# Norm and weight decoding ranked three pairs later, and new assumed durations, in the written order of an attention and MLP kernel

## The chip, the cores and the metric

The kernel runs on one core of one Trainium2 chip. The metric is the device time of one execution in microseconds (us); lower is better. Before the change it was 1068.26 us, the median of 3 runs (1066.97 to 1068.33).

## The reference

Causal attention in blocks of 64 over 8 batches, 8 heads, 576 positions and 64 values a head, followed by a norm over 512 channels and a two-layer MLP with a residual:

```python
scores = np.matmul(q, k.transpose(0, 1, 3, 2)) / np.sqrt(D)
scores = np.where(pos[:, None] // 64 >= pos[None, :] // 64, scores, -1e9)
attn = np.exp(scores - scores.max(-1, keepdims=True))
attn = attn / (attn.sum(-1, keepdims=True) + 1e-09)
x = (attn @ v).transpose(0, 2, 1, 3).reshape(B, S, 512)
xn = (x - mean(x)) / np.sqrt(var(x) + 1e-06) * g_ln
out = x + np.maximum(xn @ w_ch1, 0.0) @ w_ch2      # 512 -> 2048 -> 512
```

Everything is float32. The MLP weights come to the core as 64-bit words.

## The kernel before, in words

**Attention.** The 64 combinations of batch and head are worked as 32 pairs of two heads. A pair loads `raw` (q and k, L385) and `v` (L386). TensorE makes the scores (L396); VectorE masks them, takes the row minimum and writes them to SBUF (`soften`, L411); ScalarE takes the exponential (L414); TensorE transposes the result (L423); VectorE or ScalarE copies the transposes out of PSUM as `pt` (L217 and L215, the two branches of one helper); TensorE multiplies with `v` (L429, L433); VectorE turns the product (`ot`, L506) and SyncE stores it to `xd` (L508). The first 64 positions of eight pairs are worked together by `first` (L543 to L586), once in eight pairs. At the end of each batch `recip` (L515, L516) inverts the sums.

**Norm.** `norm_tiles` takes two 128x512 tiles of `x` at a time. For each it loads four parts from `xd` (L621, L627), multiplies them by the inverted sums (L636, on VectorE or GpSimd), stores the tile to `xrow` (L640), and takes mean and variance (`stats`, L645, L646). For both together it computes the inverse root (`guess` on VectorE, L654 to L657; `newton` on GpSimd, L663 to L666). Then the tile is centred (L671), multiplied by `g_sb` on GpSimd (L674), transposed (L676), stored to `xw` in four parts (L680) and loaded back as `xt` (L684).

**Decoding.** `decode` loads a block of weight words (`wr`, L325 and L327), rebuilds the floats on ScalarE (L330, L335), GpSimd (L333) and VectorE (L339, L342) and stores them: those of the first layer to `w1f` (L358), those of the second, split into a high and a low part, to `wcs` (L354). There are 16 blocks of each layer.

**MLP.** The 36 tiles of 128 rows are worked in rounds of 8, 8, 8, 8 and 4. In a round, 8 groups of weights follow each other. A group's first layer is seven products (L814), which TensorE works from `xm` (seven operand arrays, made in `operands`, L701 and L712) and from the weight tiles `wa` and `wb`. ScalarE copies a product out (`t`, L822), VectorE adds another to it (L827), ScalarE and VectorE write the high and the low part of the rectified result `h` (L833, L834). The second layer is one job of six matmuls and six more for each tile (`y`, L874, with the weights `wc`); VectorE adds it to `ya` (L883). In the first round a group's `wa` and `wb` are made from `w1f`: SyncE loads `wf` (L765), GpSimd makes sums and differences (`sum`, L773), ScalarE, VectorE and GpSimd split them (L784; copies at L215 and L217), and SyncE stores them to `was` and `wbs` for the later rounds (L792). `wc` is loaded from `wcs` (L758). In this text group 7 is the last of the first round. The operands of the second round overwrite those of the first, each after its last product of group 7 has read it.

**What sets the order.** Nothing runs when it is ready: the order of each of the five engines is written once, at build time, and every engine then works its instructions strictly in that order. `Plan.run` keeps a list of tasks with assumed durations. On each engine it takes, of the tasks whose inputs and buffers it believes ready, the one of the lowest `prio`. Pair k has `prio` 100 + 10k and a little more. A block of decoding has that of pair 12 + 0.97n (n counts the blocks), a norm step of the first round that of pair 10 + 3q, the operands of the first round that of pair 22, the norm of the second round that of pair 31.2, the MLP's own vector work 0 or 1, the operands of later rounds 2. SyncE issues every transfer, and so is such an engine too. A transfer is believed to land after its bytes at `BW`, a `LAG` and a `TAIL`. Buffers come from shared pools with a limit for each name: `x`, a norm tile, has 2 of the 21 places of the pool `small`.

Of the kernel before, what the change touches and what calls it, by code (L numbers as in the profile page):

```python
# [18 lines left out]
P = 128  # L19
LATS = {'PE': .2, 'ACT': .23, 'DVE': .21, 'POOL': .13, 'SP': 0}  # L20
SWITCH = {64: .2, 128: .1, 1: .05, 2: .15}
OWN = {'PE': .0, 'ACT': .2, 'DVE': .2, 'POOL': .1, 'SP': 0}
BW, LAG, TAIL = 3.0e5, .65, 1.5
BIAS = {'PE': 0, 'SP': 0, 'DVE': 0, 'ACT': 0, 'POOL': 0}
# [4 lines left out]
D_0, D_1 = 12.0, .97  # L29
LN_0, LN_1 = 10, 3  # L30


# [150 lines left out]
def attn_mlp_kernel(ctx: ExitStack, tc: tile.TileContext, qk, qk0, v, v0, w1, w2, g, out):  # L183
# [91 lines left out]
    new_mag, new_sgn = (small(n, [P, 512], I32, 2) for n in ("mag", "sgn"))  # L275
    new_ya, new_x, new_xnt = (small(n, [P, 512], F32, k) for n, k in (("ya", 10), ("x", 2), ("xnt", 2)))
    new_t, new_tt, new_sum = small("t", [P, 512], F32, 4), small("tt", [P, 2, 2, P], F32, 4), small("sum", [P, 2, 256], F32, 2)
# [97 lines left out]
    def pair(k):  # L375
# [135 lines left out]
        if c == 3:  # L511
            rs, whole = Buf(), sums_all[:, b].rearrange("p i c h -> p (i c h)")

            def recip():
                nc.vector.tensor_scalar_add(whole, whole, 1e-9)  # L515
                nc.vector.reciprocal(whole, whole)  # L516
            add("DVE", .4, recip, r=batch_sums[b], w=[rs], prio=pr())
            xparts[b].append(rs)
# [79 lines left out]
    for j in range(NJ):  # L598
        for second in (False, True):
            decode(j, second, 100 + 10 * (D_0 + D_1 * n), [ends[min(int(D_0 + D_1 * n) - 3, NPAIR - 1)]])  # L600
            n += 1
# [7 lines left out]
    def norm_tiles(n, q, prio, gate):  # L609
# [4 lines left out]
        for h in range(2):  # L614
            t = FROM[n] + ROUNDS[n] // 2 * h + q
            m, r = divmod(t, 9)
            x = new_x()
            part = [Buf(parent=x) for _ in range(4)]
# [25 lines left out]
            def stats(x=x, st=st, h=h):  # L644
                nc.vector.bn_stats(out=st.t[:, 0:6], in_=x.t)  # L645
                nc.vector.bn_aggr(out=norm.t[:, 2 * h:2 * h + 2], in_=st.t[:, 0:6])  # L646
            add("DVE", .85, stats, r=part, w=[mv, st], prio=prio)
            mvs.append(mv)
# [3 lines left out]
        def guess():  # L652
# [4 lines left out]
            nc.vector.tensor_scalar(out=yi, in0=yi, scalar1=-1, scalar2=0x5f3759df, op0=ALU.mult, op1=ALU.add)  # L657
        add("DVE", .45, guess, r=mvs, w=[seed], prio=prio)

# [229 lines left out]
    for n in range(len(ROUNDS)):  # L889
        for q in range(ROUNDS[n] // 2):  # L890
            norm_tiles(n, q, 100 + 10 * (LN_0 + LN_1 * q) if n == 0 else END + 2 * n - 10,
                       gate if n else [ends[int(LN_0 + LN_1 * q) - 2]])
        operands(n, 100 + 10 * (LN_0 + LN_1 * 4) if n == 0 else 2)
        for gp in range(GROUPS):
# [64 lines left out]
```

## Time and profile before

| | before |
|---|---|
| median of 3 runs | 1068.26 us |
| the profiled execution's own time | 1064.36 us |
| its span, first to last instruction | 1062.6 us |
| granted TensorE clock, mean | 0.998 |
| TensorE busy | 1044.1 us (98%) |
| VectorE busy | 786.5 us (74%) |
| ScalarE busy | 450.4 us (42%) |
| GpSimd busy | 294.9 us (28%) |
| moved by DMA | 248.91 MB, 234 GB/s |

The span is the time between the first and the last instruction in one profiled execution; that execution's own time is 1.76 us longer, and the median of the unprofiled runs 3.90 us longer than that. In the lines of the profile PE is TensorE, PEld its loading of weights, DVE VectorE, ACT ScalarE, POOL GpSimd and SP SyncE (SPq: its queue of transfers). "out<-in" names the tiles, "x6" counts instructions. Square brackets hold the idle time of an engine before an instruction and what ended it.

### The profile page before, as it was taken

How to read it: one execution, taken by the hardware profiler on the slowest of the kernel's cores; microseconds unless marked ns; L12 is line 12 of the kernel's file. 1: busy time of each engine (PE TensorE's matmuls, PEld its weight loads, DVE VectorE, ACT ScalarE, POOL GpSimd, SP SyncE). 2: the span in 40 equal slices, each digit the busy share in tenths (PEclk: the TensorE clock that was granted, in tenths of full speed). 3: DMA queues.
4: the chain of work that ended last, by engine and by line, in shares of the span. 5: the costliest groups of instructions: out<-in, count | busy, mean ns of one | idle time of the engine just before them, and what ended most of it. 6: DMA issues, size and time to landing. Idle time of an engine off the chain costs nothing.

```text
span 1062.6 us, 17838 instructions
## 1 busy us (share of the span) xinstructions
PE 1044.1 (98%) x6240; PEld 841.2 (79%) x6240; DVE 786.5 (74%) x1724; ACT 450.4 (42%) x1101; POOL 294.9 (28%) x442
## 2 busy tenths in 40 slices
PE   9999999999999999989999999999999999999998
PEld 6777767667678888778888888888888888888897
DVE  6878998998988899795676694676686665465554
ACT  7768979879864333242121141122133112222221
POOL 0002546533535766270222240221221220000000
PEclk9999999999999999999999999999999999999999
DMA  5448898998969898877777657778657775436873
GB/s 189 154 135 242 224 286 285 294 297 286 336 221 325 252 321 292 255 231 255 207 233 235 202 185 243 232 206 259 185 176 238 264 203 211 163 109 217 317 282 125
DMA packets 237930, 248.91 MB, mean 234 GB/s; under 512 B 159376, under 2 KB 188048, under 8 KB 227600
## 3 DMA queue, kind: packets, MB, share of 16 engines
q1 hardware_dynamic: 237840, 247.77, 71.7%
q8 instruction: 49, 0.80, 0.3%
q14 instruction: 41, 0.34, 0.1%
HBM read 182.71 MB, written 65.01 MB: 233 GB/s over the span
## 4 chain that ended last, share of the span: by engine, by line
PE 63%; DVE 2%; DMA 1%; POOL 0%; issue 0%; DVEq 0%
PE y L874 34%; PE p L814 29%; DMA wc<-wcs 1%; DVE ya L883 0%; DVE t L827 0%; DVE h L834 0%; DVE xm L712 0%; POOL x L674 0%; POOL tt L701 0%; DVE xnt L676 0%; DVE wb L784 0%; DVE tt L701 0%; POOL wb L784 0%; DVE xm L217 0%; POOL xm L712 0%
## 5 line engine op out<-in xcount | busy, mean ns | idle before, releaser
L874 PE MATMUL y<-wc,h 128*128 128x512 f32 x1728 | 434.1, 390 | 1.0 <-ACT h L833 0.8
L874 PEld LDWEIGHTS y<-wc,h 128*128 128x128 f32 x1728 | 321.8, 188 | 68.0 <-DVE h L834 1.8
L883 DVE TENSOR_TENSOR ya<-y,ya 128x512 f32<-128x512 f32 x288 | 197.0, 685 | 152.0 <-PE y L874 150.1
L814 PE MATMUL p<-xm,wa 128*128 128x512 f32 (+1 forms) x960 | 221.4, 368 | 0.0
L814 PEld LDWEIGHTS p<-xm,wa 128*128 128x128 f32 x960 | 170.0, 188 | 31.7 <-ACT sgn L335 0.2
L833 ACT ACTIVATE h<-t 128x512 fp32r<-128x512 f32 (+1 forms) x120 | 62.3, 580 | 276.2 <-DVE t L827 265.9
L814 PE MATMUL p<-xm,wb 128*128 128x512 f32 (+1 forms) x720 | 166.2, 368 | 2.7 <-DVE wb L784 2.5
L814 PEld LDWEIGHTS p<-xm,wb 128*128 128x128 f32 x720 | 127.5, 188 | 27.3 <-DVE wb L784 3.0
L822 ACT COPY t<-p 128x512 f32<-128x512 f32 (+1 forms) x120 | 65.4, 545 | 193.3 <-PE p L814 182.2
L827 DVE TENSOR_TENSOR t<-p,t 128x512 f32<-128x512 f32 (+1 forms) x120 | 75.8, 632 | 42.8 <-PE p L814 38.9
L396 PE MATMUL s<-raw 64*128 64x192 f32 (+4 forms) x640 | 96.4, 435 | 2.1 <-DMA raw<-qk 1.4
L414 ACT ACTIVATE pab<-pab,nm 128x576 f32<-128x576 f32 (+1 forms) x128 | 91.4, 722 | 9.0 <-DVE nm L411 8.8
L396 PEld LDWEIGHTS s<-raw 64*128 64x128 f32 x640 | 60.7, 186 | 38.8 <-issue 29.1
L411 DVE CUSTOM_DVE_ANT_0 pab<-s,never 128x576 f32<-128x576 f32 (+1 forms) x128 | 83.6, 682 | 3.4 <-PE s L396 3.0
L414 ACT ACTIVATE pu<-pu,nm 128x320 f32<-128x320 f32 (+1 forms) x128 | 64.3, 505 | 38.8 <-DVE nm L411 38.7
L433 PE MATMUL o<-pt,v 128*64 128x256 f32 (+1 forms) x768 | 80.3, 344 | 0.0
L333 POOL TENSOR_SCALAR mag<-mag 128x512 f32<-128x512 f32 x32 | 51.2, 1603 | 102.8 <-ACT mag L330 100.9
L834 DVE SCALAR_TENSOR_TENSOR h<-t,h 128x512 fp32r<-128x512 f32 (+1 forms) x120 | 75.4, 675 | 4.7 <-ACT h L833 4.6
L433 PEld LDWEIGHTS o<-pt,v 128*64 128x64 f32 x768 | 56.9, 137 | 26.0
L423 PE MATMUL tr<-ident,pab 128*128 128x128 f32 x512 | 66.1, 279 | 4.9 <-DVE nm L411 2.6
L215 ACT COPY pt<-tr 128x512 f32<-128x512 f32 (+1 forms) x126 | 65.0, 579 | 3.1 <-PE tr L423 2.7
L423 PEld LDWEIGHTS tr<-ident,pab 128*128 128x128 f32 x512 | 57.2, 142 | 9.8 <-DVE pt L217 3.3
(89 smaller groups left out, 982.5 us busy)
## 6 DMA issues: line engine op xcount, KB each, us to landing
wc<-wcs SPq DMA_DIRECT2D x40, 1024.0 KB, 6.7
wa<-was SPq DMA_DIRECT2D x32, 1024.0 KB, 6.6
wb<-wbs SPq DMA_DIRECT2D x32, 768.0 KB, 5.9
raw<-qk SPq DMA_DIRECT2D x32, 576.0 KB, 4.9
wr<-w SPq DMA_DIRECT2D x32, 512.0 KB, 6.5
v<-v SPq DMA_DIRECT2D x32, 320.0 KB, 5.4
x<-xd SPq DMA_DIRECT2D x144, 64.0 KB, 3.5
xrow<-x SPq DMA_DIRECT2D x36, 256.0 KB, 3.8
```

The source lines that it names most:

```text
L215: e.copy(out=out, in_=in_)
L396: nc.tensor.matmul(x, raw.t[HALF[h], 0, col], raw.t[HALF[h], 1, at:at + x.shape[1]], start=True, stop=True)
L411: add("DVE", dve(n) + .01, lambda: nc.vector.tensor_tensor_reduce(out=p.t[:, part(i, h)], in0=s.t[:, cols], in1=hide, scale=-0.125, scalar ...
L414: add("ACT", act(n, True) + .14, lambda: nc.scalar.activation(out=p.t[:, part(i, h)], in_=p.t[:, part(i, h)], func=AF.Exp, bias=nm.t[:, at ...
L423: nc.tensor.transpose(o.t[:, n * P:(n + 1) * P], x, ident)
L433: nc.tensor.matmul(o.t[HALF[h], at + lo:at + 256], v_sb.t[:, ck, HALF[h]], rhs(h), start=False, stop=(n == len(steps) - 1), skip_group_che ...
L814: nc.tensor.matmul(x.t[:, 0:TN], w_(l), xs[m].t[:, 0:half, o, k], start=start and k == e == 0, stop=k == 1 and e == 2, skip_group_check=True)
L822: add("ACT", act(TN), lambda: nc.scalar.copy(out=t.t[:, 0:TN], in_=x.t[:, 0:TN]), r=[r], w=[new], prio=0)
L827: add("DVE", dve(TN), lambda: nc.vector.tensor_add(t.t[:, 0:TN], x.t[:, 0:TN], t.t[:, 0:TN]), r=r, w=[new], prio=0)
L834: add("DVE", dve(TN), lambda: nc.vector.scalar_tensor_tensor(out=x.t[:, 1, 0:TN], in0=src(), scalar=0.0, in1=x.t[:, 0, 0:TN], op0=ALU.max, ...
L874: nc.tensor.matmul(yb.t, x.t[:, l, at:at + P], wc.t[:, i, o], start=i == e == 0, stop=i == 1 and e == 2)
L883: add("DVE", dve(512), lambda yb=yb, ya=ya: nc.vector.tensor_add(ya.t, yb.t, ya.t), r=[part, before_], w=[now], prio=1)
```

## The change

Three constants of the planner, three assumed durations and one buffer change. No instruction of the computation is added or removed.

```diff
-BW, LAG, TAIL = 3.0e5, .65, 1.5
+BW, LAG, TAIL = 3.0e5, .65, 2.5
...
+LATER = 3
...
-    new_ya, new_x, new_xnt = (small(n, [P, 512], F32, k) for n, k in (("ya", 10), ("x", 2), ("xnt", 2)))
+    new_ya, new_x, new_xnt = (small(n, [P, 512], F32, k) for n, k in (("ya", 10), ("x", 3), ("xnt", 2)))
+    new_x0 = small("x0", [P, 512], F32, 2)
...
-            add("DVE", .4, recip, r=batch_sums[b], w=[rs], prio=pr())
+            add("DVE", .89, recip, r=batch_sums[b], w=[rs], prio=pr())
...
-            decode(j, second, 100 + 10 * (D_0 + D_1 * n), [ends[min(int(D_0 + D_1 * n) - 3, NPAIR - 1)]])
+            decode(j, second, 100 + 10 * (D_0 + D_1 * n + LATER), [ends[min(int(D_0 + D_1 * n) - 3, NPAIR - 1)]])
...
-            x = new_x()
+            x = new_x() if n else new_x0()
...
-            add("DVE", .85, stats, r=part, w=[mv, st], prio=prio)
+            add("DVE", .94, stats, r=part, w=[mv, st], prio=prio)
...
-        add("DVE", .45, guess, r=mvs, w=[seed], prio=prio)
+        add("DVE", .62, guess, r=mvs, w=[seed], prio=prio)
...
-            norm_tiles(n, q, 100 + 10 * (LN_0 + LN_1 * q) if n == 0 else END + 2 * n - 10,
+            norm_tiles(n, q, 100 + 10 * (LN_0 + LN_1 * q + LATER) if n == 0 else END + 2 * n - 10,
                        gate if n else [ends[int(LN_0 + LN_1 * q) - 2]])
-        operands(n, 100 + 10 * (LN_0 + LN_1 * 4) if n == 0 else 2)
+        operands(n, 100 + 10 * (LN_0 + LN_1 * 4 + LATER) if n == 0 else 2)
```

A block of decoding and a norm step of the first round rank three pairs later; what they wait for is unchanged. The order takes a transfer to land 1 us later, and `recip`, `stats` and `guess` to take longer. The norm tiles of the first round have two buffers of their own (`x0`), those of later rounds three (`x`). Below, a line number of the changed kernel is two higher than that of the same line before.

Since nearly every row of the written order moves, three places are shown.

**VectorE in the fourteenth pair**, where the second tile of the second norm step is multiplied (L636; `pu` and `pab` are the scores of a pair, `xm` the operands, `ot` the turned result). Before:

```order
L636 TENSOR_TENSOR x_1511<-x_1511,sums_all_73 128x512
L712 TENSOR_TENSOR xm6_1693<-tt_1546,xm6_1693 128x256
L645 BN_STATS st_1700<-x_1511 128x6
L646 BN_AGGR norm_1659<-st_1700 128x2
L506 STREAM_TRANSPOSE ot_1666<-o_1665 128x512
L654 TENSOR_SCALAR norm_1659<-norm_1659 128x2
L656 TENSOR_SCALAR norm_1659<-norm_1659 128x2
L657 TENSOR_SCALAR norm_1659<-norm_1659 128x2
L411 ISA pu_1730,nm_1731<-s1_1706,never_79 128x320
```

The same tile in the changed kernel:

```order
L413 ISA pu_1813,nm_1814<-s1_1784,never_79 128x320
L413 ISA nm_1814 128x1
L413 ISA pu_1813,nm_1814<-s1_1784,never_79 128x192
L413 ISA nm_1814 128x1
L638 TENSOR_TENSOR x0_1693<-x0_1693,sums_all_73 128x512
L413 ISA pab_1838,nm_1814<-s_1800,never_79 128x576
L413 ISA nm_1814 128x1
```

The multiplication has moved behind the first scores (`pu`) of its pair; before, those stood behind it and behind the tile's statistics.

**SyncE at the end of the first round**, from the last store of first-layer weights (`w1f`) to the load of group 7 (`wf`). Before:

```order
L358 DMA w1f_4997<-sgn_5153 128x512
L680 DMA xw_5230<-xnt_5217 32x16x32 x4
L680 DMA xw_5261<-xnt_5232 32x16x32 x3
L758 DMA wc_5277<-wcs_4645 128x2048
...
L627 DMA x_5292<-xd_1119 32x16x32 x4
L627 DMA x_5314<-xd_1728 32x16x32 x4
L684 DMA xt_5290<-xw_5261 128x4x128
L792 DMA wbs_5336<-wb_5228 128x1536
L765 DMA wf_5345<-w1f_4997 128x1024
```

The same piece in the changed kernel:

```order
L360 DMA w1f_5133<-sgn_5273 128x512
L642 DMA xrow_5347<-x_5203 128x512
L356 DMA wcs_5235<-wd_5342 128x1024
L686 DMA xt_5318<-xw_5267 128x4x128
L682 DMA xw_5425<-xnt_5415 32x16x32 x4
L767 DMA wf_5463<-w1f_5133 128x1024
```

The last `w1f` store now stands behind the last tiles' loads, and between it and `wf` only the last norm step's own stores and loads are left. From the first load of `wc` on, the queue holds 12 loads of `wr` where it held 10.

**TensorE at the end of the first round** (`p<-xm,wa` and `p<-xm,wb` are products, six matmuls each; `y` a tile of the second layer, six matmuls; the numbers of `xm` name the operands). Before, the last tile of group 5's second layer, then groups 6 and 7:

```order
L874 MATMUL y<-wc,h 128x512 x24
L814 MATMUL p<-xm_1540,wa 128x512 x6
L814 MATMUL p<-xm_1559,wa 128x512 x6
L814 MATMUL p<-xm_1626,wa 128x512 x6
L874 MATMUL y<-wc,h 128x512 x18
L814 MATMUL p<-xm_1623,wa 128x512 x6
L814 MATMUL p<-xm_1688,wb 128x512 x6
L814 MATMUL p<-xm_1693,wb 128x512 x6
L874 MATMUL y<-wc,h 128x512 x6
L814 MATMUL p<-xm_1704,wb 128x512 x6
L874 MATMUL y<-wc,h 128x512 x6
```

In the changed kernel:

```order
L876 MATMUL y<-wc,h 128x512 x54
L816 MATMUL p<-xm_1772,wa 128x512 x6
L816 MATMUL p<-xm_1775,wa 128x512 x6
L816 MATMUL p<-xm_1791,wa 128x512 x6
L816 MATMUL p<-xm_1793,wb 128x512 x6
L816 MATMUL p<-xm_1808,wb 128x512 x6
L816 MATMUL p<-xm_1781,wa 128x512 x6
L816 MATMUL p<-xm_1896,wb 128x512 x6
L876 MATMUL y<-wc,h 128x512 x18
```

All eight tiles of group 6 now stand ahead of group 7's products, which follow each other without a tile between them; the first tile of group 7 comes right behind the last product. On VectorE the low parts of group 7's results, which that tile reads, stand here in the changed kernel (`xm3` is the operand that the last product reads):

```order
L218 CAST xm3_1896<-tt_4891 128x256
L218 CAST xm3_1896<-tt_5315 128x256
L836 SCALAR_TENSOR_TENSOR h_5660<-t_5578,h_5660 128x512
L836 SCALAR_TENSOR_TENSOR h_5665<-t_5606,h_5665 128x512
L836 SCALAR_TENSOR_TENSOR h_5670<-t_5591,h_5670 128x512
L836 SCALAR_TENSOR_TENSOR h_5674<-p_5558,h_5674 128x512
```

Before, the first of them stood in front of the operands that the last product reads, and the last split of group 7's `wb` stood behind nineteen rows, nearly all of operand work:

```order
L712 TENSOR_TENSOR xm5_1626<-tt_5135,xm5_1626 128x256
L883 TENSOR_TENSOR ya_2808<-y_5549,ya_2808 128x512
L701 TENSOR_TENSOR tt_5368<-xt_5290 128x256
L701 TENSOR_TENSOR tt_4801<-xt_4665,tt_4801 128x256
L701 TENSOR_TENSOR tt_5368<-xt_5290,tt_5368 128x256
L883 TENSOR_TENSOR ya_2819<-y_5568,ya_2819 128x512
L784 TENSOR_TENSOR wb_5464<-sum_5458,wb_5464 128x2x256
```

In the changed kernel that split stands ahead of the first operand.

## The prediction

> **What bounds the kernel now.** I read the page first, for its span and the engines' shares.
>
> ```profile
> span 1062.6 us, 17838 instructions
> PE 1044.1 (98%) x6240; PEld 841.2 (79%) x6240; DVE 786.5 (74%) x1724; ACT 450.4 (42%) x1101; POOL 294.9 (28%) x442
> ```
>
> TensorE is the bound; it idles 18.5 us in all, and the change takes no matmul away. The second view says where the idle time lies: busy time by stretch. The columns behind the stretch are its length, the busy time of PE, PEld, DVE, ACT and POOL with counts, the granted clock, the DMA share and GB/s. The stretches are the loaded part of attention, the first round up to group 5, its end, and the rest.
>
> ```profile
> 100.00:313.00 213.00, 204.13 (x1934) 149.99 (x1929) 195.36 (x560) 184.76 (x504) 103.02 (x134) 0.99 0.87 278
> 313.00:440.00 127.00, 126.82 (x572) 103.54 (x567) 108.11 (x179) 46.08 (x84) 70.48 (x87) 1.00 0.88 280
> 440.00:475.00 35.00, 31.44 (x135) 24.77 (x134) 32.58 (x65) 14.26 (x34) 23.06 (x31) 1.00 0.81 275
> 475.00:1050.00 575.00, 575.00 (x2688) 482.26 (x2687) 367.94 (x674) 131.74 (x271) 94.40 (x183) 1.00 0.67 219
> ```
>
> From 475 on TensorE never waits, so rounds two to five have nothing to give; only attention (8.9 us idle) and the end of the first round (3.6 us) do. Third, the waits: what TensorE waited for, us in total, times, the longest; first those in attention, then those of 440 to 475.
>
> ```profile
> PE tr L423 <- DVE nm L411: 2.6, 4, 1.4
> PE tr L423 <- DVE norm L654: 1.6, 1, 1.6
> PE s L396 <- DMA raw<-qk: 1.4, 2, 1.0
> ```
>
> ```profile
> PE p L814 <- DVE wb L784: 2.5, 1, 2.5
> PE y L874 <- ACT h L833: 0.8, 1, 0.8
> PE p L814 <- DVE t L827: 0.2, 1, 0.2
> ```
>
> None is long. So the change can only move waits of a few us; it can't touch the 1044 us of work.
>
> **Attention.** The order of TensorE in time (start, length, what, in brackets the idle time before it) shows one disturbed pair, the fourteenth, which holds the norm wait.
>
> ```profile
> 131.27 2.91 PE L396 MATMUL s<-raw 64*128 64x320 f32 x20
> ...
> 136.40 0.66 PE L423 MATMUL tr<-ident,pu 128*128 128x128 f32 x4 [1.64 <-DVE norm L654]
> 137.63 3.83 PE L423 MATMUL tr<-ident,pab 128*128 128x128 f32 x16 [0.57 <-DVE nm L411]
> ...
> 144.57 2.91 PE L396 MATMUL s<-raw 64*128 64x320 f32 x20
> ...
> 153.87 2.91 PE L396 MATMUL s<-raw 64*128 64x320 f32 x20
> 157.64 1.91 PE L423 MATMUL tr<-ident,pab 128*128 128x128 f32 x16
> ...
> 162.66 2.91 PE L396 MATMUL s<-raw 64*128 64x320 f32 x20
> ```
>
> From scores to scores this pair took 144.57 - 131.27 = 13.30 us, a quiet one 162.66 - 153.87 = 8.79: a loss of 4.5. It holds 1.64 and 0.57 of waiting, and sixteen transposes that took 3.83 instead of 1.91. The next rows say why: VectorE's row before that wait, with its idle time, then a stretch just behind it.
>
> ```profile
> 133.90 0.69 DVE L636 TENSOR_TENSOR x<-x,sums_all 128x512 f32<-128x512 f32 x1 [2.89 <-DMA x<-xd]
> ```
>
> ```profile
> 137.00:140.00 3.00, 2.33 (x12) 1.68 (x12) 3.00 (x13) 2.42 (x9) 2.10 (x12) 0.65 1.02 379
> ```
>
> VectorE stood 2.89 us before the multiplication of a norm tile whose load had not landed, with the next scores' `soften` behind it in its queue, and TensorE behind that; then the granted clock was 0.65. The order of the change takes this away: the tile's multiplication stands behind the `pu` scores. The price is -4.5. What may be late next is the same load in its new place, since its last three parts and a store of the other tile are issued only after the first tile's multiplication. The rows for it: issue and landing of these loads, and what VectorE does between the two multiplications (groups: count, busy, mean ns).
>
> ```profile
> L627 SPq DMA_DIRECT2D x<-xd x13: 422/579/2472, 117.4 to 159.9; - x13
> DMA to landing us min/median/max: 2.7/5.2/9.5
> ```
>
> ```profile
> L411 DVE CUSTOM_DVE_ANT_0 pab<-s,never 128x576 f32<-128x576 f32 x86 | 56.0, 680 | 0.5 <-PE s L396 0.5
> L411 DVE CUSTOM_DVE_ANT_0 pu<-s,never 128x320 f32<-128x320 f32 x84 | 31.1, 415 | 1.7 <-PE s L396 1.7
> L217 DVE COPY pt<-tr 128x512 f32<-128x512 f32 (+1 forms) x42 | 27.0, 670 | 0.9 <-PE tr L423 0.7
> L506 DVE STREAM_TRANSPOSE ot<-o 128x512 f32<-128x512 f32 x22 | 15.6, 707 | 10.0 <-PE o L433 10.0
> ```
>
> Between them stand, by the written order, four `pab` (4 x 0.680), four `pu` (4 x 0.415), two `pt` (2 x 0.670), one `ot` (0.707), the statistics and seven operand instructions. The first four kinds come to 6.4 us; the other nine (two of statistics) I estimate at 0.4 each, about the mean `pu`, so 3.6, and 10.0 in all. Of these the issues of a store and three loads take 4 x 0.58 = 2.3, so the load has 7.7 us to land. The median 5.2 fits, the slowest, 9.5, is 1.8 late. I take 1.0, about half, so -4.5 + 1.0 = **-3.5**. Ends: -5.9, if the `raw` waits (1.4) go as well and nothing is late; and +2.9, if two of the other moved tiles are each 1.8 late and each costs the half-clock transposes again (3.83 - 1.91 = 1.92): 2 x 3.7 - 4.5.
>
> The ten `pt` copies that go from VectorE to ScalarE, the two fewer `sgn` steps on VectorE and the multiplications that go to GpSimd I cost at nothing: TensorE is busy 204 of 213 us there and so covers them; uncovered, a copy costs its 0.67.
>
> **End of the first round: what goes.** In the change the last split of `wb` stands ahead of the operands, and eight tiles of group 6 stand together, so the waits of 2.5, 0.8 and 0.2 go: **-3.5**, with little doubt, as the place of each is gone.
>
> **End of the first round: group 7's weights.** TensorE's first row of it, one tile's time and the transposition of a norm tile from the chain of waits, SyncE's issues, and GpSimd's rows:
>
> ```profile
> 453.79 4.24 PE L814 MATMUL p<-xm,wa 128*128 128x512 f32 x18
> ```
>
> ```profile
> 444.39 1.36 PE y L874 x6
> ...
> 455.86 0.71 DVE xnt L676
> ```
>
> ```profile
> 334.89 0.60 SPq L327 DMA_DIRECT2D wr<-w  x1
> 344.80 0.43 SPq L327 DMA_DIRECT2D wr<-w  x1
> 439.55 0.43 SPq L765 DMA_DIRECT2D wf<-w1f  x1
> 454.70 0.32 SPq L792 DMA_DIRECT2D was<-wa  x1
> ```
>
> ```profile
> 446.28 0.20 POOL L663 TENSOR_TENSOR norm<-norm 128x2 f32<-128x2 f32 x1 [0.51 <-DVE norm L657]
> 450.87 0.74 POOL L773 TENSOR_TENSOR sum<-sum,wf 128x256 f32<-128x256 f32 x1
> ```
>
> Before, `wf` was issued at 439.55 and `wa` was whole at 454.70, 15.15 later; 4.6 of these (446.28 to 450.87) a `newton` stood between two sums of GpSimd. In the change the sums follow one another, so 10.55. But `wf` comes later. Two more blocks are loaded in this stretch, which moves the last store ahead of it by at least the least spacing of two first-layer loads, 344.80 - 334.89 = 9.9; and `wf` now stands behind the store of the first tile of the last norm step, whose transposition ran at 455.86 to 456.57, 17.0 behind `wf`, though the third `x` buffer brings that forward. I take the middle of 9.9 and 17.0, 13.5. Then `wa` is whole at 439.55 - 3.5 + 13.5 + 10.55 = 460.1. TensorE is there, after five more tiles, at 453.79 - 3.5 (attention) - 0.8 (the wait for `h`) + 5 x 1.36 + 1.0 (the crowding below) = 457.3. It waits **+2.8**; with 9.9 not at all, with 17.0 for 6.3.
>
> **End of the first round: nothing between.** All seven products follow each other and group 7's first tile comes right behind. Before, two tiles of group 6 covered the way from product to tile. Now VectorE has two casts and three low parts to do in between, all bare:
>
> ```profile
> L834 DVE SCALAR_TENSOR_TENSOR h<-t,h 128x512 fp32r<-128x512 f32 x24 | 20.3, 884 | 0.3 <-ACT h L833 0.2
> L834 DVE SCALAR_TENSOR_TENSOR h<-p,h 128x512 fp32r<-128x512 f32 x8 | 5.4, 676 | 0.0
> L217 DVE CAST xm<-tt 128x256 fp32r<-128x256 f32 x7 | 1.7, 281 | 0.0
> ```
>
> 2 x 0.281 + 3 x 0.884 = **+3.2**. With the fourth low part too it is 3.9, with all at 0.676 it is 2.6. By the same rows reading two SBUF tiles costs 0.2 more than reading one from PSUM. The Trainium skill, SBUF — State Buffer, Who interferes with whom, says that a VectorE instruction with two SBUF inputs contends with a GpSimd instruction that reads SBUF; GpSimd is busy 23 of 35 us there, so the trace agrees, and were GpSimd idle at this place the term would be 2.6.
>
> Behind a wait of 1.64 and one of 0.57, with transposes alone between, the clock fell (above) and cost 1.92. Behind the wait of 2.5 at the end of the round the stretch's granted clock stays 1.00. I take half, **+0.9**, between 0 and 1.9. The Trainium skill, TensorE: Matmul & The Clock Gate, Part 1, says that the gate halves the clock after about 3.4 us of idling, in a window that runs freely, and elsewhere on it (Part 4: PE-mode transpose) that transposes don't count as busy in the same way as matmuls. Both fit the rows (136.40 to 137.63 held transposes alone); by that rule a bare wait of 3.2 is just too short and the sum below is 0.0 and not +0.9.
>
> **Crowding.** Seven products of group 4 and three of group 5 also follow each other, so their PSUM tiles are emptied in a row by ScalarE and VectorE. The nearest rows are the 0.8 and 0.2 above: **+1.0**, between 0 and 2.
>
> **Sum.** -3.5 - 3.5 + 2.8 + 3.2 + 0.9 + 1.0 = +0.9. The profiled execution took 1064.36 us itself, 1.76 more than its span; so 1065.3. The median of the runs, 1068.26, lies 3.9 above that execution, so the median becomes 1069.2.
>
> **Rivals.** 0.2% (2.1 us) is about what a measurement of this kernel can tell from no change: 1066.1 to 1070.4.
>
> Faster: `wf` isn't later. Before, its place behind the norm's loads in SyncE's queue held it, not its data; with a third `x` buffer those loads go early. And the moved tiles land in time. Then -5.9 - 3.5 + 0 + 3.2 + 0 + 1.0 = -5.2: 1063.1. For it: 7.7 us against a median landing of 5.2. Against it: DMA is busy 0.87 in attention, and 9.5 was seen. It decides if `wf` is issued before 439.55 - 3.5 + 9.9 = 445.9.
>
> Slower: two moved tiles land late in attention, in front of scores, because their loads stand behind a store that waits for VectorE. Then +2.9 - 3.5 + 2.8 + 3.2 + 0.9 + 1.0 = +7.3: 1075.6. It decides once a multiplication of a norm tile waits over 1.8 us twice; the row of 2.89 shows that it can happen, the median that it needn't.
>
> That the order doesn't do what it says: the norm's gates are unchanged, so a step that was bound by its loads stays where it is. Then the waits only change places and the time stays within the 0.2%; this is part of the forecast's case.
>
> **Chances.** The forecast's case has 0.38; its own range is that of the wait for group 7's weights, 0 to 6.3 where I took 2.8: 1066.4 to 1072.7 (of the 0.38, 0.28 lie within 0.2%, 0.08 above, 0.02 below). The faster rival has 0.35, its mechanism being the one with a median row behind it; the slower 0.27, since it needs two loads near the slowest seen. So 0.37 faster, 0.28 the same, 0.35 slower. The range reaches a little over a us past both rivals' times, 1063.1 and 1075.6: 1062 to 1077. All ends at once (-6.8 and +13.5, so 1061.5 and 1081.8) would be wider, and I leave them out.
>
> **What would show it.** Right: the pair from 131 takes 9 to 10 us; no wait for `wb` at the end of the first round; one for group 7's `wa` or `wf` of up to 6, and one of 2.6 to 3.9 for `h` before its first tile; TensorE without waits after that. Wrong: `wf` issued no later than now; new idle time before L638 in attention; or a wait in rounds two to five, on which I have put nothing, since their order is hardly moved.

## The result and the profile after

The changed kernel takes 1076.99 us, the median of 6 runs (1073.76 to 1080.93); the kernel before took 1067.62 (6 runs). The ratio is 1.0095, with a 95% interval of 1.0076 to 1.0113: it is slower by 0.95%. The forecast was 1069.2, no change within 0.2%. The time lies just inside the upper end of the range (1077), near the rival that was slower (1075.6), and only half by that rival's way.

The profiled execution after took 1076.56 us, 1.86 more than its span. The page's first lines, then the stretches of the prediction and one more at the end of the first round:

```profile
span 1074.7 us, 17803 instructions
PE 1050.5 (98%) x6240; PEld 844.7 (79%) x6240; DVE 787.4 (73%) x1712; ACT 452.8 (42%) x1107; POOL 297.3 (28%) x448
```

```profile
100.00:313.00 213.00, 201.49 (x1880) 147.25 (x1880) 189.79 (x551) 177.10 (x486) 93.35 (x125) 0.98 0.83 263
313.00:440.00 127.00, 125.01 (x591) 101.05 (x588) 111.25 (x181) 52.89 (x102) 74.01 (x91) 1.00 0.91 297
440.00:475.00 35.00, 35.00 (x155) 28.78 (x155) 31.49 (x66) 10.74 (x22) 17.55 (x25) 1.00 0.82 259
475.00:1050.00 575.00, 570.00 (x2632) 476.06 (x2631) 370.05 (x665) 135.47 (x279) 109.20 (x201) 0.99 0.67 219
476.00:490.00 14.00, 9.00 (x28) 6.56 (x27) 12.83 (x21) 5.77 (x15) 11.33 (x13) 0.76 0.52 208
```

TensorE idles more in attention (11.5 us between 100 and 313, 8.9 before) and for 5.0 of the 14 us between 476 and 490, where it idled not at all before. Its busy time also grew by 6.4 us for the same matmuls; the mean granted clock fell from 0.998 to 0.994, which I estimate at some 4 us of it (0.004 of 1050). To split the loss I compare when the same work starts. First TensorE's scores of the second half of attention, then group 7:

```profile
178.46 2.91 PE L398 MATMUL s<-raw 64*128 64x320 f32 x20
...
184.69 3.63 PE L425 MATMUL tr<-ident,pab 128*128 128x128 f32 x16 [2.29 <-DVE nm L413]
...
192.05 3.17 PE L398 MATMUL s<-raw 64*128 64x320 f32 x20
...
218.32 1.99 PE L398 MATMUL s<-raw 64*128 64x320 f32 x12
...
306.61 2.91 PE L398 MATMUL s<-raw 64*128 64x320 f32 x20
```

```profile
468.08 4.24 PE L816 MATMUL p<-xm,wa 128*128 128x512 f32 x18
...
479.22 0.73 PE L876 MATMUL y<-wc,h 128*128 128x512 f32 x2 [1.46 <-ACT h L835]
483.50 6.26 PE L876 MATMUL y<-wc,h 128*128 128x512 f32 x16 [3.54 <-DVE h L836]
489.60 2.67 PE L816 MATMUL p<-xm,wa 128*128 128x512 f32 x11
```

The last pair's scores begin at 306.61; before, at this place:

```profile
300.38 2.91 PE L396 MATMUL s<-raw 64*128 64x320 f32 x20
```

So attention lost 6.2 us between these two executions. Four kernels further down keep the change's order up to there (early, cover, wf, wforder); in their profiles the last pair begins at 307.3 to 308.8, so the loss is no accident of one execution. The three pairs from 178.46 to 218.32 alone lost 8.3: they took 39.9 us, and 38.2 to 40.0 in those four kernels, where the same pairs took 31.5 before (181.63 to 213.16). Group 7's first product starts at 468.08 and started at 453.79: 14.3 later, of which 6.8 are the five more tiles ahead of it, so 7.5 lost by then and 1.3 of them in the first round. From that product to the second round's first one (489.60) pass 21.5 us, which hold seven products and three tiles (13.6): 7.9 lost. Before, the second round began here:

```profile
473.44 1.52 PE L814 MATMUL p<-xm,wa 128*128 128x512 f32 x6
```

That is 19.65 us with seven products and five tiles (16.3): 3.3 lost. The sum is 6.2 + 1.3 + 4.6 = 12.1 us, the whole difference of the two spans. The prediction had -3.5 for attention and, for the rest, -3.5 + 2.8 + 3.2 + 0.9 + 1.0 = +4.4 where 5.9 were measured. Attention is the term with the wrong sign.

VectorE's two multiplications of the third norm step show what held up the pair at 178.46, which took 13.59 us:

```profile
176.85 0.69 DVE L638 TENSOR_TENSOR x<-x,sums_all 128x512 f32<-128x512 f32 x1
182.46 0.69 DVE L638 TENSOR_TENSOR x<-x,sums_all 128x512 f32<-128x512 f32 x1 [2.81 <-DMA x<-xd]
```

It is the stall of before, one norm step later: 2.81 us for a tile's load, the `pu` scores behind it in VectorE's queue, TensorE behind those, then transposes at a lower clock (3.63 us for sixteen instead of 1.91; the granted clock was 0.54 from 184.6 to 188.3).

### The profile page after: what moved, and what is told of

The parts are those of the page before. It is cut to its first block, busy times and chain, and to the rows that moved or that the text cites. A ratio compares the mean times of both kernels' runs of the same rounds, so it can differ in the third digit from the quotient of the medians.

```text
span 1074.7 us, 17803 instructions
## 1 busy us (share of the span) xinstructions
PE 1050.5 (98%) x6240; PEld 844.7 (79%) x6240; DVE 787.4 (73%) x1712; ACT 452.8 (42%) x1107; POOL 297.3 (28%) x448
## 4 chain that ended last, share of the span: by engine, by line
PE 84%; DVE 9%; DMA 2%; issue 2%; POOL 1%; SPq 1%; ACT 1%; DVEq 0%; POOLq 0%; ACTq 0%
PE y L876 33%; PE p L816 29%; PE s L398 7%; PE tr L425 6%; PE o L435 5%; PE o L431 2%; DVE pab L413 1%; DMA x<-xd 1%; DVE h L836 1%; DMA xw<-xnt 1%; DVE ya L885 1%; DVE xm L714 1%; DVE pu L413 1%; DVE pt L218 1%; DVE sgn L341 1%
## 5 line engine op out<-in xcount | busy, mean ns | idle before, releaser
L885 DVE TENSOR_TENSOR ya<-y,ya 128x512 f32<-128x512 f32 x288 | 197.1, 686 | 169.1 <-PE y L876 166.0
L398 PE MATMUL s<-raw 64*128 64x512 f32 (+4 forms) x640 | 98.3, 439 | 2.6 <-DVE ot L508 1.3
L398 PEld LDWEIGHTS s<-raw 64*128 64x128 f32 x640 | 61.9, 189 | 39.9 <-issue 30.0
L216 ACT COPY pt<-tr 128x512 f32<-128x512 f32 (+1 forms) x136 | 70.4, 584 | 8.3 <-PE tr L425 8.1
L425 PEld LDWEIGHTS tr<-ident,pab 128*128 128x128 f32 x512 | 58.3, 144 | 14.3 <-ACT pt L216 3.6
```

Source lines behind the costliest of these rows:

```text
L216: e.copy(out=out, in_=in_)
L398: nc.tensor.matmul(x, raw.t[HALF[h], 0, col], raw.t[HALF[h], 1, at:at + x.shape[1]], start=True, stop=True)
L425: nc.tensor.transpose(o.t[:, n * P:(n + 1) * P], x, ident)
L885: add("DVE", dve(512), lambda yb=yb, ya=ya: nc.vector.tensor_add(ya.t, yb.t, ya.t), r=[part, before_], w=[now], prio=1)
```

## The experiments

Eighteen kernels were timed in five rounds each, beside the kernel before on the same chip. In nine of them the planner's written order stays and a few rows of it are moved by hand; in these, line numbers are 57 higher than in the kernel they come from.

**Moving the late tile (tile).** The first theory was that waits like the one above make the loss, each at its place. VectorE's rows, `-` where they stood and `+` where they stand now:

```
-L638 TENSOR_TENSOR x0_2177<-x0_2177,sums_all  (with its statistics and the guess)
 L413 ISA pu  (four)
 L413 ISA pab 128x576
 L413 ISA pab 128x448
+L638 TENSOR_TENSOR x0_2177<-x0_2177,sums_all  (with its statistics and the guess)
```

> The changed kernel with one move in VectorE's written order: in the pair that begins at 178.5 us the multiplication of the third norm step's second tile, its statistics and the step's guess stand behind the first two pab scores instead of ahead of the pu scores. Theory A (the disturbed pair of 13.6 us is VectorE standing 2.8 us for a load with the scores queued behind it): the pair shrinks to 9 to 10 us, no wait before that multiplication, 4 to 5 us less in all, about 1072.5. Rival (VectorE and ScalarE are simply full there, and the load only marks where it shows): the pair keeps 12 us or more, or the next pairs grow by as much, and the time stays within 1.5 us of the changed kernel's 1077.0.

Measured: 1076.96, ratio 1.0092 (1.0075 to 1.0110); nothing gained, as the rival had it. TensorE's rows of the same pairs:

```profile
181.63 2.91 PE L455 MATMUL s<-raw 64*128 64x320 f32 x20
...
193.41 2.91 PE L455 MATMUL s<-raw 64*128 64x320 f32 x20 [2.29 <-DMA raw<-qk]
199.14 0.63 PE L482 MATMUL tr<-ident,pab 128*128 128x128 f32 x4 [1.79 <-DVE nm L470]
...
219.80 2.74 PE L455 MATMUL s<-raw 64*128 64x320 f32 x15
```

The wait for the tile is gone and one of 2.29 for the next pair's `raw` is there: its load stands on SyncE behind the store to `xrow` that waits for the moved multiplication. The pair took 11.78 us instead of the 9 to 10 expected, and the three pairs 219.80 - 181.63 = 38.2; in the changed kernel 218.32 - 178.46 = 39.9, and as little as 38.2 in a kernel whose order is the change's up to there (wf).

**Moving the next load too (tile2).** The tile stands behind the four `pu` scores, and on SyncE:

```
+L387 DMA raw_2319<-qk 128x1152
 L642 DMA xrow_2269<-x0_2131 128x512
 L388 DMA v_2284<-v 128x640
 L510 DMA xd_2164<-ot_2239 128x512
 L642 DMA xrow_2306<-x0_2177 128x512
-L387 DMA raw_2319<-qk 128x1152
```

> The changed kernel with two moves in the pair that begins at 178.5 us: on VectorE the late tile's multiplication, its statistics and the guess stand behind the four pu scores, on SyncE the load of the next pair's raw stands ahead of the two stores to xrow that wait for the multiplications. Theory A, mended after the first run (the tile's load and the next raw load, which stood behind a store that waits for the multiplication, are late together): no wait for raw, pairs of 9 to 10.5 and 11 us, 3 to 5 us less, about 1073. Rival (the queues of DMA are full in this stretch, so that one of these loads lands late in whatever order): a wait of 2 us or more stays at raw or at the tile, and the gain is under 1.5 us.

Measured: 1077.71, ratio 1.0100 (1.0076 to 1.0124).

```profile
179.99 2.91 PE L455 MATMUL s<-raw 64*128 64x320 f32 x20
...
191.84 2.91 PE L455 MATMUL s<-raw 64*128 64x320 f32 x18 [1.15 <-DVE ot L565]
197.87 0.63 PE L482 MATMUL tr<-ident,pab 128*128 128x128 f32 x4 [1.97 <-DVE nm L470]
...
219.77 2.75 PE L455 MATMUL s<-raw 64*128 64x320 f32 x16
```

`raw` waits 0.44 us and the three pairs still take 39.8. Now `ot` and the next scores wait for VectorE, and the time is the rival's again. The stretch takes 38 to 40 us whichever load is late, against 31.5 before. Removing a single wait has gained nothing here.

**Group 7's results earlier (early).** Two high parts on ScalarE and two low parts on VectorE move up:

```
 L829 TENSOR_TENSOR t_5591<-p_5558,t_5591 128x512
+L836 SCALAR_TENSOR_TENSOR h_5665<-t_5606,h_5665 128x512
+L836 SCALAR_TENSOR_TENSOR h_5670<-t_5591,h_5670 128x512
 L714 TENSOR_TENSOR xm6_1808<-tt_4891,xm6_1808 128x256
...
 L836 SCALAR_TENSOR_TENSOR h_5660<-t_5578,h_5660 128x512
-L836 SCALAR_TENSOR_TENSOR h_5665<-t_5606,h_5665 128x512
-L836 SCALAR_TENSOR_TENSOR h_5670<-t_5591,h_5670 128x512
```

> The changed kernel with two of group 7's results moved up: on ScalarE the high parts of the two that the first tile reads stand ahead of four operand casts, on VectorE their low parts stand behind the second addition of t, ahead of operand work. Nothing is put between products and tile on TensorE. Theory A (the time before that tile goes to operand work that stands ahead of the results, slowed by GpSimd, and to the halved clock behind it): the waits of 1.5 and 3.5 us fall to under 1.5 together, the clock stays whole, 6 to 8 us less, about 1070. Theory B (without a tile between, TensorE must wait for the whole way from product to result): the waits stay above 3 us and the gain is under 3 us.

Measured: 1076.60, ratio 1.0096 (1.0081 to 1.0112).

```profile
478.97 4.66 PE L933 MATMUL y<-wc,h 128*128 128x512 f32 x18
485.50 0.50 PE L873 MATMUL p<-xm,wa 128*128 128x512 f32 x1 [1.88 <-DVE xm L275]
486.44 3.19 PE L873 MATMUL p<-xm,wa 128*128 128x512 f32 x6 [0.43 <-DVE xm L771]
```

The first tile no longer waits at all, so theory B (it must, without a tile between) is wrong. But the 6 to 8 us of theory A aren't there either: the second round's products wait instead, for the operands that were pushed back, and run at half clock (3.19 us for six instead of 1.52; granted clock 0.50 from 486.4 to 490).

**The cover back (cover).** Two tiles of group 6 go behind group 7's sixth and seventh product, as before:

```
-L876 MATMUL y<-wc,h 128x512 x54
+L876 MATMUL y<-wc,h 128x512 x42
 L816 MATMUL p<-xm x36
+L876 MATMUL y<-wc,h 128x512 x6
 L816 MATMUL p<-xm_1896,wb 128x512 x6
-L876 MATMUL y<-wc,h 128x512 x18
+L876 MATMUL y<-wc,h 128x512 x24
```

> The changed kernel with two tiles of group 6's second layer moved behind group 7's sixth and seventh product, as in the kernel before, their additions on VectorE with them. Theory A: TensorE reaches group 7 2.7 us sooner, waits there about 2 us for its weights, which came 0.6 us before it needed them, and keeps half of the wait before the first tile of group 7; 1 to 4 us less, 1073 to 1076. Theory B (the missing cover is the cause): the wait before that tile is under 1 us, the clock stays whole and 7 us or more are gained, about 1069.5.

Measured: 1076.48, ratio 1.0084 (1.0067 to 1.0101): neither theory's gain. The tile waits nearly as long as it did, until nearly the same time:

```profile
483.11 6.80 PE L933 MATMUL y<-wc,h 128*128 128x512 f32 x16 [3.31 <-DVE h L893]
```

TensorE's order changed and the moment hardly did: VectorE sets it.

**Tile and early together (both).**

> The changed kernel with the moves of the first and second run of this call together. Theory A: the two gains add up, 10 to 13 us, 1064 to 1067, which is level with the kernel before or better. Rival (crowding that only changes place): less than 7 us together, above 1070.

Measured: 1077.55, ratio 1.0094 (1.0075 to 1.0113). The gains don't add up, since there were none.

**Group 7 as before, with its weights earlier (wforder, wf).** SyncE's load of `wf` goes ahead of the four `xw` stores (both kernels), and TensorE gets the order of before around group 7 (the first one only):

```
 L686 DMA xt_5318<-xw_5267 128x4x128
+L767 DMA wf_5463<-w1f_5133 128x1024
 L682 DMA xw_5425<-xnt_5415 32x16x32 x4
-L767 DMA wf_5463<-w1f_5133 128x1024
```

> The changed kernel with group 7's order of the kernel before put back by hand: SyncE's load of group 7's wf stands ahead of the four stores that wait for the last step's transposition, three of group 7's products stand behind three tiles of group 6 and not eight, and of the other five tiles three stand behind the third product, one behind the sixth, one behind the seventh. Theory C (after the first three runs: the second round's operands can only be made once group 7's products have read the first round's, this work fills VectorE and GpSimd for some 17 us, and late weights let TensorE use up its cover of eight tiles ahead of it): wf goes out at 447 to 450 instead of 456, the waits and the half clock between 470 and 490 fall from 8 to under 3 us, 5 to 8 us less, 1069 to 1072. Rival (the last norm step itself is late, so the second round's operands are late whatever the order is): the waits move to the first products of the second round, gain under 2 us.

> The changed kernel with only SyncE's load of group 7's wf moved ahead of the four stores that wait for the last step's transposition; TensorE's order is as it was. Theory C: the weights come 8 us sooner and nobody uses them sooner, because all eight tiles of group 6 still stand ahead; within 1.5 us of the changed kernel's 1077. Rival (late weights as such, by what their splits push back on VectorE): 3 us less or more, 1074 or below.

Measured: 1075.86, ratio 1.0082 (1.0058 to 1.0105), and 1078.38, ratio 1.0099 (1.0077 to 1.0121). Theory C said 5 to 8 us for the first; at most 2 are there, within the noise, as the rival had it, and the load went out at 452.38, not at 447 to 450. The second is within the 1.5 us of theory C. With the order of before TensorE waits in both places:

```profile
465.12 0.73 PE L873 MATMUL p<-xm,wa 128*128 128x512 f32 x2 [1.67 <-DVE wa L275]
...
485.63 0.96 PE L933 MATMUL y<-wc,h 128*128 128x512 f32 x3 [1.00 <-DVE h L893]
```

The weights are loaded 4 us earlier and then wait for VectorE to split them.

**Wforder and tile2 together (all3).**

> The changed kernel with the moves of the first and the third run of this call together. If both theories hold, the gains add up: 8 to 13 us less, 1064 to 1069, level with the kernel before. By the rivals under 4 us, above 1073.

Measured: 1074.56, ratio 1.0074 (1.0050 to 1.0098): 2.4 us less than the changed kernel, where the two theories asked for 8 to 13 and the rivals for under 4. None of the rows moved here can be blamed alone. So the next runs undo whole parts of the change.

**Ranks alone and durations alone (rank, times).** The kernel before with the three `+ LATER` (decoding, norm steps, the first round's operands), and the kernel before with `TAIL` 2.5 and the durations of `recip`, `stats` and `guess`.

> The kernel before with the three later ranks alone (LATER = 3 for decoding, norm and first operands); assumed durations and buffers as before. Theory D (after the first six runs: VectorE's work is put off out of attention, its busy time up to 313 us falls from 271.9 to 262.3 us, and comes back at the end of the first round, where VectorE is full): most of the loss is here, 1073 to 1077; VectorE's busy time up to 313 us falls by 5 us or more, and TensorE loses 5 us or more between group 7's products and the second round. Rival E (the longer assumed landing and the buffers made the poor order): within 2 us of 1067.

> The kernel before with the four assumed durations alone (landing 1 us later, recip, stats and guess longer); ranks and buffers as before. Theory D: within 2 us of 1067, VectorE's busy time up to 313 us within 3 us of 271.9. Rival E: 1072 or more.

Measured: 1090.07, ratio 1.0206 (1.0187 to 1.0224), and 1083.19, ratio 1.0147 (1.0131 to 1.0163). Each alone is worse than all parts together. What TensorE waited for at the second round's first products, ranks alone, then durations alone:

```profile
PE p L815 <- DVE xm L218: 16.8, 1, 16.8
```

```profile
PE p L814 <- DVE xm L712: 8.1, 1, 8.1
PE p L814 <- DVE xm L217: 2.3, 1, 2.3
```

Neither theory fits both: the first is slow as theory D had it (and slower than its 1077), the second as rival E had it. VectorE's busy time up to 313 us was 267.3 and 265.3, in the wrong order for theory D, and 264.4 in a kernel further down that is as fast as before (later0), so D is given up.

**The buffers (later0, nobuf).** `LATER = 0` in the changed kernel; and the changed kernel with two `x` and no `x0`.

> The changed kernel with LATER = 0: assumed durations and buffers of the change, ranks of before. Theory F (the third x buffer lets the last norm step load early; without it the second round's operands are late, which is the wait of 8 to 17 us for xm in the runs with durations alone and ranks alone): no wait over 3 us for xm at the second round's first products, 1063 to 1070. Rival (the longer assumed landing makes a poor order by itself): 1075 or more.

> The changed kernel with the buffers of before (two x, no x0). Theory F: the second round's first products wait 5 us or more for xm, 1081 or more. Rival (buffers do nothing, the durations and ranks mend each other): within 3 us of 1077 and no such wait.

Measured: 1066.81, ratio 0.9995 (0.9981 to 1.0009), and 1086.50, ratio 1.0182 (1.0165 to 1.0199). With the buffers the durations cost nothing; without them the changed kernel is 9.5 us slower still, waiting 4.7 us for `xm` at the second round's first products and 5.4 for `t` at a product of group 7, so theory F holds in its main part. The buffers matter apart from the ranks too: with the ranks of before, the durations without them (times) took 16.4 us more than with them (later0). The buffers alone were not run.

**Which rank (dec, nrm, opnd, steps).** The changed kernel, with the later rank for some parts only. For dec:

```diff
-            norm_tiles(n, q, 100 + 10 * (LN_0 + LN_1 * q + LATER) if n == 0 else END + 2 * n - 10,
+            norm_tiles(n, q, 100 + 10 * (LN_0 + LN_1 * q) if n == 0 else END + 2 * n - 10,
...
-        operands(n, 100 + 10 * (LN_0 + LN_1 * 4 + LATER) if n == 0 else 2)
+        operands(n, 100 + 10 * (LN_0 + LN_1 * 4) if n == 0 else 2)
```

opnd undoes the first of these lines, steps the second, nrm only the one of `decode`.

> The changed kernel with the later rank for decoding only; norm and first operands have the rank of before. Theory D: part of the loss, 1069 to 1074, since decoding's VectorE steps are only part of what is put off. If the norm's lateness alone makes the end of the first round (late last step, late second operands), it is within 2 us of 1067.

> The changed kernel with the later rank for norm and first operands only; decoding has the rank of before. Theory D: the rest of the loss, 1069 to 1074. If decoding alone makes it (late weights of group 7), it is within 2 us of 1067 and wf of group 7 goes out within 3 us of 440.

> The changed kernel with the later rank for decoding and first operands, the norm steps at the rank of before. If the late norm steps make the loss (VectorE's norm work put off out of attention): within 3 us of the run with decoding alone, 1060 to 1066. If the operands' rank makes it: 1070 or more.

> The changed kernel with the later rank for decoding and norm steps, the first operands at the rank of before. Theory G (the last norm step and group 7's weights are late together, so group 7's products and the second round's operands come late): the loss stays, 1074 to 1079, the last operand load of the second round goes out at 470 or later (463.5 before, 472.1 in the changed kernel). If the operands' rank makes the loss by itself (the run with decoding and operands was 7 us slower than decoding alone): 1070 or less.

| later rank for | kernel | median, us | ratio, 95% interval | last pair begins |
|---|---|---|---|---|
| nothing | later0 | 1066.81 | 0.9995 (0.9981 to 1.0009) | 306.7 |
| decoding | dec | 1062.53 | 0.9947 (0.9931 to 0.9963) | 298.54 |
| decoding, operands | opnd | 1069.48 | 1.0019 (1.0008 to 1.0031) | 299.94 |
| norm steps, operands | nrm | 1075.90 | 1.0080 (1.0054 to 1.0106) | 311.47 |
| decoding, norm steps | steps | 1082.78 | 1.0156 (1.0132 to 1.0180) | 317.34 |
| all three | the change | 1076.99 | 1.0095 (1.0076 to 1.0113) | 306.61 |

All three kernels with late norm steps are slow, all three without them lie between 1062.5 and 1069.5. The norm steps' rank costs 7.5 us from opnd to the change and 20 from dec to steps. Its size was not foreseen: dec came out below both its expectations, nrm above both (its `wf` at 447.79), opnd just under its second and steps 3.8 us above theory G's. Every one of these ranks moves nearly every row, so these are prices of whole orders; that they all point one way is what speaks for the norm steps. The last pair's scores, for dec, opnd, nrm and steps:

```profile
298.54 2.91 PE L398 MATMUL s<-raw 64*128 64x320 f32 x20
```

```profile
299.94 2.91 PE L398 MATMUL s<-raw 64*128 64x320 f32 x20
```

```profile
311.47 2.91 PE L398 MATMUL s<-raw 64*128 64x320 f32 x20
```

```profile
317.34 2.91 PE L398 MATMUL s<-raw 64*128 64x320 f32 x20
```

Most of the price is paid in attention: 6.7 us between opnd and the change, 18.8 between dec and steps. Profiles of one attention order differ by up to 4 us (tile 308.20, both 304.32), so the first of these is near that noise, and the second is far above it. Attention alone doesn't rank the kernels: later0 begins the last pair as late as the change does and needs 757.9 us from there to the end of its span, where the change needs 768.1. The rest shows in the last loads of the second round's operands (`xt`) and of group 7's `wf`: the change, then dec, then steps.

```profile
456.43 0.51 SPq L767 DMA_DIRECT2D wf<-w1f  x1
...
472.07 0.37 SPq L686 DMA_DIRECT2D xt<-xw  x1
```

```profile
413.49 0.79 SPq L767 DMA_DIRECT2D wf<-w1f  x1
...
465.89 0.38 SPq L686 DMA_DIRECT2D xt<-xw  x1
```

```profile
476.31 2.46 SPq L686 DMA_DIRECT2D xt<-xw  x2
```

With late norm steps the second round's operands are loaded at 472 and 476, with decoding alone at 466; and there, though decoding is just as late in rank, group 7's weights go out 43 us earlier than in the change. In steps the loss stays without the operands' rank, and their rank even softens it when the steps are late.

A late tile load, as at 182.46, is not the only way: in nrm no multiplication of a norm tile on VectorE waits for its load before the last pair (GpSimd stands once for one, 3.82 us), and this pair still begins 11.1 us later than before. TensorE's largest sum of waits there, up to 315 us, was for VectorE's scores (7.4 us in nrm, 2.6 before):

```profile
PE tr L425 <- DVE nm L413: 7.4, 5, 2.5
```

VectorE had other work in front of these scores, operands and weights among it.

**Decoding later with the old durations (decold).** The kernel before with the buffers and the decoding's rank.

> The kernel before with the buffers of the change and the later rank for decoding, assumed durations as before. If the measured durations carry part of the gain of decoding alone: 1065 or more. If buffers and the decoding's rank do it without them: within 2 us of 1062.5.

Measured: 1067.49, ratio 1.0005 (0.9992 to 1.0018). The gain of dec needs the longer durations as well; durations and buffers without the rank (later0) give nothing either. dec is the fastest kernel of all: 0.5% faster than the kernel before (interval 0.9931 to 0.9963) and 14.5 us faster than the change.

**The prices of the two waits of before (bfix).** The kernel before, VectorE's rows:

```
-L636 TENSOR_TENSOR x_1511<-x_1511,sums_all  (with its statistics and the guess)
 L411 ISA pu  (four)
 L411 ISA pab 128x576
+L636 TENSOR_TENSOR x_1511<-x_1511,sums_all  (with its statistics and the guess)
...
+L784 TENSOR_TENSOR wb_5464<-sum_5458,wb_5464 128x2x256
 L217 CAST xm0_1540<-xt_4665 128x256
...
-L784 TENSOR_TENSOR wb_5464<-sum_5458,wb_5464 128x2x256
```

> The kernel before with two moves on VectorE: in the fourteenth pair the late tile's multiplication, its statistics and the guess stand behind the first pab score, and group 7's last wb split stands ahead of the operands. If the prediction's two terms for these waits were right as prices (4.5 and 2.5): 4 to 7 us less than before, 1060 to 1063. If another wait takes their place, as it did for the moved tile of the changed kernel: within 2 us of 1067.

Measured: 1067.36, ratio 1.0003 (0.9988 to 1.0018).

```profile
132.81 2.91 PE L453 MATMUL s<-raw 64*128 64x320 f32 x20
...
143.76 2.91 PE L453 MATMUL s<-raw 64*128 64x320 f32 x20
...
472.17 2.92 PE L871 MATMUL p<-xm,wb 128*128 128x512 f32 x6 [3.05 <-DVE t L884]
```

The fourteenth pair falls from 13.30 to 10.95 us, but the last pair begins 168.5 us after it (at 301.34) and did so 169.1 before: of the 2.35 gained in the pair 0.6 are left. The pair from 161.78 alone takes 1.2 us more than the one from 162.66 did. The wait of 2.54 for `wb` is replaced by one of 3.05 for `t`.

## Why the prediction was wrong, step by step

- **Attention, -3.5: the step that failed.** "The order of the change takes this away" was right for that pair, which begins at 131.83 now and takes 9.86 us. "The price is -4.5" was wrong. bfix took the same wait out and left the rest of attention's order: 0.6 of it remained in attention, and none in the time of the whole kernel (ratio 1.0003). My reading is that VectorE and the loads are nearly full in this stretch (VectorE busy 195 of 213 us, DMA 0.87), so the next thing is late instead. The working let the same load cost 1.0 in its new place, and at its upper end two other tiles be 1.8 late; one was, the next step's, by 2.81, and removing that wait (tile) gained nothing either. The upper end, +2.9, was below the 6.2 measured, since the term counted stalls of one kind at known places and took the norm steps' rank as neutral. The runs show that this rank costs 7.5 or 20 us, with the other parts fixed.
- **The waits that go, -3.5: right as to the waits, wrong as a gain.** None of the three is there. In bfix the largest is followed by another of its size when its cause is removed.
- **Group 7's weights, +2.8: both halves were off and cancelled.** `wf` went out 16.9 us later, at the end of the range I gave (17.0), and TensorE came there not at 457.3 but at 468.08, 0.6 us behind the weights. No wait: that is luck, made by the loss in attention.
- **Nothing between, +3.2 and +0.9: right mechanism, too small.** The waits are 1.46 and 3.54, and the sixteen matmuls behind them took 6.26 us instead of 16 x 0.227 = 3.6: 7.6 in all. I counted two casts and three low parts; VectorE also had a `tt` there, and GpSimd worked beside all of them:

```profile
478.77 0.95 DVE L703 TENSOR_TENSOR tt<-xt,tt 128x256 f32<-128x256 f32 x1
...
479.64 1.54 DVE L218 CAST xm<-tt 128x256 fp32r<-128x256 f32 x2
...
481.11 3.47 DVE L836 SCALAR_TENSOR_TENSOR h<-t,h 128x512 fp32r<-128x512 f32 x3
```

  A cast took 0.77 where I used 0.281, a low part 1.16 where I used 0.884. By the rule of the Trainium skill on the gate (TensorE: Matmul & The Clock Gate, Part 1: half clock after about 3.4 us of idling) I had weighed a sum without the clock term; the wait was 3.54 and not 3.2, and the clock fell, which fits the rule. Other runs don't: behind 3.05 in bfix (granted clock 0.50 from 472.1 to 478), and behind 1.88 and 0.43 in early, with one matmul between, it was halved too, while behind 2.54 in the kernel before it stayed 1.00. So by these runs a bare wait of 3.2 can lower the clock, and the clock term was too small: 2.6 where I had 0.9. Early and cover show what the term was worth as a cause: nothing, since the operand work of the second round sets the moment.
- **Crowding, +1.0:** 2.0 us of idling between 313 and 440 against 0.2, so +1.8, within the bounds.
- **The rivals.** The faster one needed `wf` before 445.9; it came at 456.43. The slower one needed two multiplications waiting over 1.8 us; one did, so that its time (1075.6) was near is half luck. Neither asked whether the three ranks pull the same way. They don't: decoding alone, with the durations and buffers, would have been the faster result.

Left open: why decoding later, with durations and buffers, brings group 7's weights forward to 413.5 (with the operands' rank too, in opnd, they go out at 439.2); and by which instructions the late norm steps slow attention, beyond the pairs shown.

## What to carry to other kernels

In an order that is written ahead and worked strictly, a wait on the trace has no price until the row that causes it has been moved alone: of nine kernels with such moves here, eight ended within 1.5 us of the kernel that they came from and one (all3) gained 2.4. VectorE had 89% to 93% of its time taken at these places; that such an engine offers the next wait at once is how I read it. A change that bundles several ranks should be split before it is judged, as one of three made the gain and another more than ate it. And buffers are judged with the order that uses them: without them the change cost another 9.5 us, and the new durations alone 16.4.

## What was not expected of the hardware

The same written order took 9.63 or 13.05 us in one pair. GpSimd multiplies two tiles by `g_sb` there, beside VectorE's two `sgn` steps. Both in the changed kernel, then in tile, whose order is the same up to this place:

```profile
110.12 0.69 DVE L344 SCALAR_TENSOR_TENSOR sgn<-mag,sgn 128x512 int32<-128x512 int32 x1
110.73 0.69 DVE L341 SCALAR_TENSOR_TENSOR sgn<-wr,sgn 128x512 int32<-128x512 int32 x1
```

```profile
109.84 3.94 POOL L676 TENSOR_TENSOR x<-x,g_sb 128x512 f32<-128x512 f32 x2 [2.20 <-DVE x L673]
```

```profile
109.06 1.77 DVE L401 SCALAR_TENSOR_TENSOR sgn<-mag,sgn 128x512 int32<-128x512 int32 x1
110.76 1.75 DVE L398 SCALAR_TENSOR_TENSOR sgn<-wr,sgn 128x512 int32<-128x512 int32 x1
```

```profile
108.77 3.18 POOL L733 TENSOR_TENSOR x<-x,g_sb 128x512 f32<-128x512 f32 x2 [2.18 <-DVE x L730]
```

One of the two engines is slower each time: a `sgn` step takes 0.69 us and GpSimd's two multiplications 3.94, or 1.77 and 3.18. Of the nine profiles with this order three have the first outcome (the change, both, tile2) and six the second. In tile the 2 us lost turned into 3.4 for TensorE, which waited 1.80 for `ot` and then worked its scores at a lower clock (granted 0.63 from 113.18 to 117.69). The Trainium skill, SBUF — State Buffer, Who interferes with whom, says that the order of issue decides who is blocked. The traces don't show that order: GpSimd's record starts 0.28 us ahead of VectorE's in the changed kernel and 0.29 in tile, so what decides it here stays open.
